# One queue for the feed-forward traffic, and the last column block's gradients moved into attention

## The chip, the cores and the metric

The kernel runs on one core of a Trainium2 chip. A core has five engines that run side by side, each through its own list of instructions in order: TensorE (PE in the profile; its weight loads are PEld), VectorE (DVE), ScalarE (ACT), GpSimd (POOL) and SyncE (SP, which only issues DMAs here). An engine waits for others through semaphores. DMAs are issued by SP, ACT or POOL and carried out by 16 DMA engines. Matrix products go to PSUM, which the DMAs do not touch here: DVE or ACT copies a result out of it ("evicts" it), and until then the bank cannot take the next product.

The metric is the device time of one execution, in microseconds. Before the change it was 905.26 us, the median of three runs (904.66 to 910.99).

## The reference

The forward pass mixes two branches of one input `x` (2048 rows, 512 columns, bfloat16) by a learned gate, and the kernel returns its output and all gradients for a given `grad_out`:

```python
g = sigmoid((x * gate_w).sum(-1, keepdims=True))
a = attention(x, wqkv) @ wo      # 32 heads of 16, causal, window of 256
b = (where(gate > 0, gate, 0) * up) @ W_down   # gate = x @ W_gate, up = x @ W_up
out = g * a + (1 - g) * b
```

Outputs are `out` (out_0), the gradient of x (out_1), of wqkv (out_2), wo (out_3), W_gate (out_4), W_up (out_5), W_down (out_6) and gate_w (out_7). The feed-forward width is F = 1376, which is ten blocks of 128 columns and 96 more.

Of the feed-forward branch the backward pass needs, for each block of columns, `h` (the product of the rectified gate and up), `dg` and `du` (the gradients at gate and up), then the weight gradients x^T dg, x^T du and h^T db, where db is `grad_out` times (1 - g), and later the sums over all blocks that make `b` and the gradient of x.

## The kernel before

The kernel has three stages, all written out in Python loops; in the first two the order of instructions on each engine is the order in which the code issues them.

**Feed-forward stage** (loop at L416). A step `k` is one block of 128 columns (`fc`, 11 of them) for one quarter of the rows (`tg`, 512 rows): 44 steps. The last block starts at F - 128 = 1248, so its first 32 columns repeat those of block 9. The parts of a step are issued with lags, so that iteration n does `gate` and `up` of step n, `dh` of step n-2, `turn_h` of n-1 (L362), `keep` of `hT` of n-3 and `turn_dgu` and `keep` of `dgT`, `duT` of n-4 (L366, L371), and `weights` of n-6 (L375).

- `gate`, `up` and `dh` are four matmuls of 512 columns each (L336). ACT rectifies (`rg`, L342) and copies `dh` (L356), DVE makes `upm` (L348) and `dg` (L359), POOL makes `h` (L350) and `du` (L360). In this form columns lie on partitions and rows along the free axis.
- `turn_h` and `turn_dgu` are DMA transposes on SP that bring rows onto the partitions for the weight gradients (`h_r` of 4 blocks of 128x128, `dgu_r` of 8).
- `keep` stores `h`, `dg` and `du` to three DRAM tensors `hT_d`, `dgT_d`, `duT_d`, by three DMAs on ACT's queue (L373), for the last stage.
- `weights` is 16 matmuls of 256 columns (L383, `wps`: both x^T dg and x^T du) and 4 of 512 (L385, `dps`), accumulated over the four quarters. After the fourth, ACT evicts one half of `wps` and all of `dps`, DVE the other half (L398 to L400, through the helper at L72 and L74), and three stores go out one iteration later. There is one `wps` buffer, so the next block's gradients wait for the eviction. For the last block, results go through a tile `wst_end` that attention's pool lends.
- Between these, from iteration 9 on, `make_da` and `turn_da` scale `grad_out` by g, store it as `da_d` and turn it, one row tile an iteration for sixteen iterations, on DVE and SP; and the attention projections of the first group are issued in the last iterations (L456 to L459).

In the built program each DMA on the queues of SP and ACT also waits for an earlier DMA: eight semaphores are given out in turn to the DMAs of both queues, in the order of issue in the code.

**Attention** (loop at L924). It goes through four column groups `c` of eight heads and, in each, through 46 turns. A turn makes scores S and their gradients' products D on PE (L666), exp on ACT (L699), masks on POOL (L709), the product with D on DVE (L716), row sums BA on PE (L733, L735), turns the probabilities either on PE (L770) with a copy by DVE or ACT or by a DMA transpose on SP (L762), and makes the CD products (L492, L495). PE's other work is spread over the turns as background jobs with a price in microseconds (`bg`, `jobs`, L995 to L1017): the projections of the next quarter of rows (L146), and from group 1 on the weight gradients of the group before (`grad_parts`, L564; matmuls at L599 and L602). At the start of each quarter of a group, `jobs` adds 0, 1, 2 or 2 jobs (L944). The gradients read rows of `da_d`, in pieces of two row tiles (`load_da`, L568): the first four are loaded by SP, the next four by ACT's queue (L604).

**Last stage** (loop at L1057): for each row tile the products that give `out` and the gradient of x, from what the first two stages have left in DRAM.

The lines that carry the change:

```python
            if at(1):
                turn_h(at(1))
            if at(3):
                keep(at(3), (hT_d, at(3).hT[:]))
            if at(4):
                turn_dgu(at(4))
                keep(at(4), (dgT_d, at(4).dgT), (duT_d, at(4).duT))
            if at(6):
                f = weights(at(6))
```

Of the kernel before, what the change touches and what calls it, by code (L numbers as in the profile page):

```python
# [22 lines left out]
def kernel(  # L23
# [100 lines left out]
    pjA = ctx.enter_context(tc.tile_pool(name="pjA", bufs=1))  # L124
    pjs = {}
    pools = {}

# [71 lines left out]

    with ExitStack() as p1, tc.manual_schedule():  # L200
# [7 lines left out]
        fp = p1.enter_context(tc.tile_pool(name="ffn", bufs=4))  # L208

# [98 lines left out]
        def make_da(t):  # L308
            da_t = fp.tile([P, D], BF, tag="da_t", bufs=2, name="da_t")
            nc.vector.tensor_scalar(da_t[:], go_in[t // TPG][:, t % TPG, :], g_all[:, t:t + 1], None, op0=ALU.mult)  # L310
            nc.sync.dma_start(da_d[t * P:(t + 1) * P, :], da_t[:])
# [32 lines left out]
        def up(k):  # L344
            ups = ps1.tile([P, TGW], F32, tag="mm", bufs=3, name="ups")
            product(ups, lambda c: Wu_sb[:, c, k.fsl], lambda c: x_T[k.tg][:, c, :])
            k.upm, k.hT = tile1("upm"), tile1("hT")
            nc.vector.scalar_tensor_tensor(out=k.upm[:], in0=k.rg[:], scalar=0.0, in1=ups[:],  # L348
                                           op0=ALU.is_gt, op1=ALU.mult)
            nc.gpsimd.tensor_tensor(out=k.hT[:], in0=k.rg[:], in1=k.upm[:], op=ALU.mult)  # L350

        def dh(k):
# [4 lines left out]
            k.dgu = fp.tile([P, 2, TGW], BF, tag="dgu", name="dgu")  # L357
            k.dgT, k.duT = k.dgu[:, 0, :], k.dgu[:, 1, :]
            nc.vector.tensor_tensor(out=k.dgT, in0=dh_sb[:], in1=k.upm[:], op=ALU.mult)  # L359
            nc.gpsimd.tensor_tensor(out=k.duT, in0=dh_sb[:], in1=k.rg[:], op=ALU.mult)  # L360

        def turn_h(k):  # L362
            k.h_r = fp.tile([P, TPG, P], BF, tag="h_r", bufs=6, name="h_r")
            nc.sync.dma_start_transpose(out=k.h_r[:], in_=k.hT[:])

        def turn_dgu(k):  # L366
            k.dgu_r = fp.tile([P, 2, TPG, P], BF, tag="dgu_r", name="dgu_r")
            nc.sync.dma_start_transpose(out=k.dgu_r[:].rearrange("p a t f -> p (a t) f"),
                                        in_=k.dgu[:].rearrange("p a s -> p (a s)"))

        def keep(k, *pairs):  # L371
            for dst, src in pairs:
                nc.scalar.dma_start(dst[k.fsl, k.ts], src)  # L373

        def weights(k):  # L375
# [14 lines left out]
            if k.fc < FC - 1:  # L390
                wst = fp.tile([P, DC, 2, P], BF, tag="wst", bufs=2, name="wst")
                dst = fp.tile([P, D], BF, tag="dst", bufs=2, name="dst")
                parts = [(0, wst[:, 0:h2, :, :]), (h2, wst[:, h2:DC, :, :])]
            else:
                end = wide("wst_end")[:].rearrange("p u a h q -> p (u a h q)")
                parts = [(c0, end[:, c0 * 2 * P:(c0 + h2) * 2 * P].rearrange("p (c a f) -> p c a f", c=h2, a=2)) for c0 in (0, h2)]
                dst = end[:, 2 * D:3 * D]
            for (c0, t), eng in zip(parts, ("act", "dve")):  # L398
                evac(t, v[:, c0:c0 + h2, :, :], eng)
            evac(dst[:], acc["d"][:], "act")  # L400

            def store():
                whole = parts if k.fc == FC - 1 else [(0, wst[:])]
                for a, to in ((0, out_4), (1, out_5)):
                    for c0, t in whole:
                        nc.sync.dma_start(to[:, k.fsl].rearrange("(c p) f -> p c f", p=P)[:, c0:c0 + t.shape[1], :], t[:, :, a, :])
# [755 lines left out]
```

## Time and profile before

| | |
|---|---|
| median of three runs | 905.26 us (904.66 to 910.99) |
| the profiled execution's own time, and its span | 910.07 us, 908.3 us |
| mean granted clock of TensorE in it | 0.987 |
| feed-forward stage on PE | from the start to 257.2 us |
| attention, start of its first and last exp | 258.9 and 707.2 us |

A profile is one execution. "Span" is the time from its first instruction to its last. Rows of the timeline give start and duration in us, the engine, the line, the operation, the tiles (written <- read), the count, and in brackets the idle time of the engine ahead of the row and what ended it. Rows of groups give busy time and mean duration in ns, then idle time. A "q" behind an engine's name marks its queue issuing a DMA. Busy times of PE overlap, since matmuls are pipelined: the distance from one start to the next is what a matmul costs.

### The profile page before, as it was taken

What the parts mean: (1) busy time and instruction counts of PE and PEld (TensorE: products, weight loads), DVE (VectorE), ACT (ScalarE), POOL (GpSimd) and SP (SyncE); (2) the same over time, 40 slices, a digit from 0 to 9 for tenths busy, and PEclk for the clock granted to TensorE, in tenths of its full rate; (3) what the DMA queues carried; (4) which work ended last, traced back from release to release, by engine and by line L of the source; (5) the groups of instructions that cost most, each with busy time, mean ns of one, the idle gap of its engine ahead of it and who ended that gap; (6) DMA issues with size and microseconds to landing.
All of it is one profiled execution on the core that took longest, in us unless ns stands there. A gap on an engine that the chain in (4) does not pass through costs nothing. (4 is left out here: it accounts for less than half of the span.)

```text
span 908.3 us, 29628 instructions
## 1 busy us (share of the span) xinstructions
PE 868.0 (96%) x12569; PEld 565.9 (62%) x12569; DVE 492.5 (54%) x754; ACT 390.0 (43%) x565; POOL 474.0 (52%) x883
## 2 busy tenths in 40 slices
PE   7999999999989999999999999999899999999998
PEld 4566555565657777776777767777577744444443
DVE  4543222233237888878778777788677323232322
ACT  5522222223246767675556655667465311111111
POOL 2544444454326877876668766687566512222221
PEclk9999999999988999999999999999899999999999
DMA  9989989989725999999987999999999999778750
GB/s 279 211 184 218 218 211 198 226 202 199 194 51 78 151 136 183 138 152 236 170 116 134 138 239 160 135 164 168 197 180 203 245 253 216 180 195 195 195 125 29
DMA packets 444334, 161.25 MB, mean 178 GB/s; under 512 B 362696, under 2 KB 441896, under 8 KB 444200
## 3 DMA queue, kind: packets, MB, share of 16 engines
q1 hardware_dynamic: 418520, 133.13, 81.5%
q10 hardware_dynamic: 23856, 20.98, 8.1%
q0 software_dynamic: 1824, 5.25, 1.6%
q8 instruction: 98, 1.61, 0.7%
q14 instruction: 36, 0.29, 0.1%
HBM read 38.44 MB, written 38.41 MB: 85 GB/s over the span
## 5 line engine op out<-in xcount | busy, mean ns | idle before, releaser
L716 DVE TENSOR_TENSOR PP<-PP,D 128x1024 bf16<-128x1024 bf16 (+1 forms) x184 | 219.6, 1193 | 69.6 <-POOL PP L709 24.9
L699 ACT ACTIVATE PP<-S 128x1024 bf16<-128x1024 f32 (+1 forms) x184 | 185.2, 1006 | 96.1 <-PE D L666 47.4
L709 POOL TENSOR_SCALAR_AFFINE_SELECT PP<-PP 128x512 bf16<-128x512 bf16 (+1 forms) x188 | 143.3, 763 | 109.9 <-ACT PP L699 94.6
L74 DVE COPY p<-pt 128x1024 bf16<-128x1024 bf16 x167 | 114.4, 685 | 17.4 <-PE pt L770 17.2
L770 PE MATMUL pt<-ident,PP 128*128 128x128 bf16 x1536 | 120.0, 224 | 1.6 <-DVE p L74 0.9
L350 POOL TENSOR_TENSOR hT<-rg,upm 128x512 bf16<-128x512 bf16 x44 | 52.5, 1193 | 127.1 <-DVE upm L348 103.0
L733 PE MATMUL BA<-KV,PP 128*128 128x33 bf16 x1440 | 106.9, 180 | 6.7 <-ACT BAs L72 6.7
L383 PE MATMUL wps<-dgu_r,x_r 128*128 128x256 bf16 x704 | 105.6, 273 | 4.3 <-DVE wst L74 3.9
L733 PEld LDWEIGHTS <-PP 128*128 128x128 bf16 x1440 | 85.9, 96 | 31.8 <-issue 12.2
L735 PE MATMUL BA<-KV,PP 128*128 128x17 bf16 x1440 | 102.4, 171 | 0.5 <-issue 0.5
L492 PE MATMUL CD<-rq,p 128*128 128x32 bf16 x1440 | 95.0, 176 | 0.0
L495 PE MATMUL CD<-rq,p 128*128 128x16 bf16 x1440 | 93.7, 169 | 1.2 <-issue 1.2
L735 PEld LDWEIGHTS <-PP 128*128 128x128 bf16 x1440 | 85.0, 97 | 14.7 <-issue 10.1
L770 PEld LDWEIGHTS <-PP 128*128 128x128 bf16 x1536 | 91.2, 100 | 1.8 <-issue 1.8
L383 PEld LDWEIGHTS <-x_r 128*128 128x128 bf16 x704 | 68.8, 98 | 36.2 <-issue 5.9
L666 PE MATMUL S<-zT,K 32*128 32x128 bf16 (+3 forms) x1056 | 78.3, 241 | 5.3 <-ACT PP L699 3.3
L495 PEld LDWEIGHTS <-p 128*128 128x128 bf16 x1440 | 80.6, 96 | 1.6 <-issue 1.3
L492 PEld LDWEIGHTS <-p 128*128 128x128 bf16 x1440 | 80.8, 96 | 0.3
L666 PE MATMUL D<-zT,V 32*128 32x128 bf16 (+3 forms) x1056 | 73.4, 240 | 4.3 <-DVE PP L716 3.8
L1074 ACT COPY a_sb<-aps 128x512 f32<-128x512 f32 x16 | 9.4, 586 | 145.9 <-issue 133.1
L348 DVE SCALAR_TENSOR_TENSOR upm<-rg,ups 128x512 bf16<-128x512 bf16 x44 | 30.2, 686 | 67.6 <-PE ups L336 43.0
L385 PE MATMUL dps<-db_r,h_r 128*128 128x512 bf16 x176 | 66.7, 379 | 0.0
(144 smaller groups left out, 1471.3 us busy)
## 6 DMA issues: line engine op xcount, KB each, us to landing
dqkvo_d<-rows_st SPq DMA_DIRECT2D x14, 512.0 KB, 4.7
hT_d<-hT ACTq DMA_DIRECT2D x44, 128.0 KB, 2.2
dgT_d<-dgu ACTq DMA_DIRECT2D x44, 128.0 KB, 2.8
duT_d<-dgu ACTq DMA_DIRECT2D x44, 128.0 KB, 2.8
duT_g<-duT_d SPq DMA_DIRECT2D x8, 640.0 KB, 5.9
dgT_g<-dgT_d SPq DMA_DIRECT2D x7, 640.0 KB, 5.6
gt<-hT_d SPq DMA_DIRECT2D x7, 640.0 KB, 6.0
dar<-da_d SPq DMA_DIRECT2D x16, 256.0 KB, 5.2
```

The lines of the kernel that those rows point to most:

```text
L74: nc.vector.tensor_copy(out, in_)
L383: nc.tensor.matmul(acc["w"][:, c, :], lhsT=x_r[:, t, c * P:(c + 1) * P], rhs=k.dgu_r[:, :, i, :], start=(go_ and c % 2 == 0), stop=no_, sk ...
L385: nc.tensor.matmul(acc["d"][:], lhsT=k.h_r[:, i, :], rhs=db_r[:, t, :], start=go_, stop=no_)
L492: nc.tensor.matmul(cd[0][:, h, :], lhsT=p2[:, 0, pr, :], rhs=rq[:, h, 0:2 * Dh], start=cd[1], stop=True, skip_group_check=True)
L495: nc.tensor.matmul(cd[0][:, h, 0:Dh], lhsT=p2[:, 1, pr, :], rhs=rq[:, h, 2 * Dh:3 * Dh], start=False, stop=True, skip_group_check=True)
L666: nc.tensor.matmul(dst, lhsT=proj[(u.c, kb // TPG)][nm + ("", "1")[par]][rows[par], (kb % TPG) * P:(kb % TPG + 1) * P], rhs=proj[(u.c, qb ...
L699: nc.scalar.activation(two[:].rearrange("p x a b q -> p x a (b q)")[:, :, 0, 0:n], flat(us[0].S[:], n), ACT.Exp)
L709: nc.gpsimd.affine_select(out=out, in_=out, compare_op=ALU.is_ge, fill=0.0, base=0 if up else -1, pattern=[[0, 2], [0, b1 - b0], [1 if up ...
L716: nc.vector.tensor_tensor(out=v(1), in0=v(0), in1=flat(vs[0].D[:], n), op=ALU.mult)
L733: nc.tensor.matmul(BA[:, h, 0:33], lhsT=u.PP[:, 0, 2 * i + pr, :], rhs=kv[:, kb % TPG, h, 1:34], start=(first and pr == 0), stop=True, ski ...
L735: nc.tensor.matmul(BA[:, h, 33:50], lhsT=u.PP[:, 1, 2 * i + pr, :], rhs=kv[:, kb % TPG, h, 0:17], start=False, stop=True, skip_group_check ...
L770: nc.tensor.transpose(pt[:, a, b if u.nb == 2 else 2 * u.x + b, :], u.PP[:, a, b, :], ident[:])
```

## The change

- `h`, `dg` and `du` of a step lie in one tile `hgu` (five buffers, in a pool of its own on the right side of the memory), are turned by one DMA transpose of 12 blocks and stored by one DMA into one DRAM tensor `hgu_d`, both on SP, three iterations after the step's `gate` (`weights` stays at six).
- ACT's queue issues only the first loads: the stores above and `load_da` are on SP. The store of `da_t` is issued just ahead of its transpose, one iteration later than before.
- The last block (fc = 10) is not given to `weights`. Its `h` is turned into a tile `h_end` of attention's pool, its `dg` and `du` into four tiles `dgu_end` that share buffers with the `da` rows, and `tail_parts` makes its gradients as three background jobs in attention's group 0: `down` (16 matmuls of 512 columns) and two times `up_gate` (32 matmuls of 192 columns, for the 96 new columns of two matrices). Group 0 takes 2 jobs in its first quarter and 1 in its second.
- `db_r` and `db_T`, which the first stage makes, lie in the two buffers that attention uses for `rows_st`.
- The pool of turned blocks `P2` is opened after turn 2 of attention, in the place of the `hgu` pool, which is closed there. In the first two row tiles of group 0, the pairs from the fourth on (k >= 3) are turned by DMA instead of PE.

```diff
-    hT_d = dram.tile([F, S], BF, name="hT_d")
-    dgT_d = dram.tile([F, S], BF, name="dgT_d")
-    duT_d = dram.tile([F, S], BF, name="duT_d")
+    hgu_d = dram.tile([3, F, S], BF, name="hgu_d")
+    hT_d, dgT_d, duT_d = (hgu_d[a] for a in range(3))
...
+    def rows_tile(name):
+        return st.tile([P, NT, 4, P], BF, tag="rows_st", name=name)
...
-        db_r = ap1.tile([P, NT, D], BF, name="db_r")
-        db_T = ap1.tile([P, DC, S], BF, name="db_T")
+        db_T = rows_tile("db_T")[:].rearrange("p t a n -> p (t a n)").rearrange("p (c s) -> p c s", c=DC)
+        db_r = rows_tile("db_r")[:].rearrange("p t a n -> p t (a n)")
...
+        fl = fend.enter_context(tc.tile_pool(name="ffnl", bufs=4, side="right"))
...
         def turn_da(t):
+            nc.sync.dma_start(da_d[t * P:(t + 1) * P, :], da_in[t][:])
             nc.sync.dma_start_transpose(out=da_T[t // TPG][:, :, (t % TPG) * P:(t % TPG + 1) * P], in_=da_in[t][:])
...
+        def turn(k, a0, a1, out):
+            nc.sync.dma_start_transpose(out=out, in_=k.hgu[:, a0:a1, :].rearrange("p a s -> p (a s)"))
+
         def turn_h(k):
-            k.h_r = fp.tile([P, TPG, P], BF, tag="h_r", bufs=6, name="h_r")
-            nc.sync.dma_start_transpose(out=k.h_r[:], in_=k.hT[:])
+            if k.tg == 0:
+                acc["h"] = wide("h_end")[:].rearrange("p u a h q -> p (u a) h q")
+            k.h_r = acc["h"][:, k.tg, :, :]
+            turn(k, 0, 1, k.h_r)
 
         def turn_dgu(k):
-            k.dgu_r = fp.tile([P, 2, TPG, P], BF, tag="dgu_r", name="dgu_r")
-            nc.sync.dma_start_transpose(out=k.dgu_r[:].rearrange("p a t f -> p (a t) f"),
-                                        in_=k.dgu[:].rearrange("p a s -> p (a s)"))
-
-        def keep(k, *pairs):
-            for dst, src in pairs:
-                nc.scalar.dma_start(dst[k.fsl, k.ts], src)
+            if k.fc < FC - 1:
+                r = fp.tile([P, 3, TPG, P], BF, tag="hgu_r", name="hgu_r")
+                k.h_r, k.dgu_r = r[:, 0, :, :], r[:, 1:3, :, :]
+                turn(k, 0, 3, r[:].rearrange("p a t f -> p (a t) f"))
+            else:
+                r = gwp.tile([P, 2, D], BF, tag="dar", bufs=4, name="dgu_end")
+                k.dgu_r = r[:].rearrange("p a (t f) -> p a t f", f=P)
+                turn(k, 1, 3, r[:].rearrange("p a (t f) -> p (a t) f", f=P))
+
+        def keep(k):
+            nc.sync.dma_start(hgu_d[:, k.fsl, k.ts].rearrange("a f s -> f a s"), k.hgu[:])
...
-            if at(1):
+            if at(1) and at(1).fc == FC - 1:
                 turn_h(at(1))
-            if at(3):
-                keep(at(3), (hT_d, at(3).hT[:]))
-            if at(4):
-                turn_dgu(at(4))
-                keep(at(4), (dgT_d, at(4).dgT), (duT_d, at(4).duT))
-            if at(6):
+            for lag, end in ((3, False), (3, True)):
+                if at(lag) and (at(lag).fc == FC - 1) == end:
+                    turn_dgu(at(lag))
+                    keep(at(lag))
+            if at(6) and at(6).fc < FC - 1:
...
-                    ev.setdefault(turn + 1, []).append(("load", lambda: load_da(t0 // 2 + 4, nc.scalar)))
+                    ev.setdefault(turn + 1, []).append(("load", lambda: load_da(t0 // 2 + 4)))
...
+        def tail_parts():
+            ends = steps[-NTG:]
+            lo = FC * P - F
+            new = FC * P - lo - (FC - 1) * P
...
+                for t in range(t0, t0 + step):
+                    nc.tensor.matmul(hold["d"][:], lhsT=ends[t // TPG].h_r[:, t % TPG, :], rhs=db_r[:, t, :], start=(t == 0), stop=(t == NT - 1))
...
+                    for c in range(2):
+                        nc.tensor.matmul(hold[h][:, c, :, :], lhsT=x_r[:, t, (2 * h + c) * P:(2 * h + c + 1) * P],
+                                         rhs=ends[t // TPG].dgu_r[:, :, t % TPG, lo:P], start=(t == 0 and c == 0), stop=(t == NT - 1),
+                                         skip_group_check=True)
...
-                        u.dma = x == 0 and len(blocks) == 2 and (c > 0 or q > 0) and (c < DC - 1 or q < NT - 2)
+                        u.dma = x == 0 and len(blocks) == 2 and (c > 0 or q > 0 or k >= 3) and (c < DC - 1 or q < NT - 2)
...
-            jobs = []
+            jobs = tail_parts()
...
-                        for _ in range((0, 1, 2, 2)[j // TPG]):
+                        for _ in range(((2, 1, 0, 0) if c == 0 else (0, 1, 2, 2))[j // TPG]):
...
+                if turn == 2:
+                    fend.close()
+                    pools["p2"] = p3b.enter_context(tc.tile_pool(name="attp2", bufs=2, side="right"))
```

More of the change, by code (lines that the diff above doesn't have):

```diff
@@ L198, in project_parts @@
             return out
+    fend = ExitStack()
     with ExitStack() as p1, tc.manual_schedule():
@@ L389, in weights @@
             v = acc["w"][:].rearrange("p c (a f) -> p c a f", a=2)
[L390 to L399, printed above, removed]
+            wst = fl.tile([P, DC, 2, P], BF, tag="wst", bufs=2, name="wst")
+            dst = fl.tile([P, D], BF, tag="dst", bufs=2, name="dst")
+            for c0, eng in ((0, "act"), (h2, "dve")):
+                evac(wst[:, c0:c0 + h2, :, :], v[:, c0:c0 + h2, :, :], eng)
             evac(dst[:], acc["d"][:], "act")
             def store():
-                whole = parts if k.fc == FC - 1 else [(0, wst[:])]
                 for a, to in ((0, out_4), (1, out_5)):
-                    for c0, t in whole:
-                        nc.sync.dma_start(to[:, k.fsl].rearrange("(c p) f -> p c f", p=P)[:, c0:c0 + t.shape[1], :], t[:, :, a, :])
+                    nc.sync.dma_start(to[:, k.fsl].rearrange("(c p) f -> p c f", p=P), wst[:, :, a, :])
                 nc.sync.dma_start(out_6[k.fsl, :], dst[:])
@@ L937 @@
                     if j == 0:
-                        sts[c] = st.tile([P, NT, 4, P], BF, tag="rows_st", name="rows_st")
+                        sts[c] = rows_tile("rows_st")
                     if j % TPG == 0:
```

53 lines of the change are left out of this document (39 added, 14 removed).

## The prediction

> **What bounds the kernel now.** I read the page first: busy shares and the granted clock.
>
> ```profile
> PE 868.0 (96%) x12569; PEld 565.9 (62%) x12569; DVE 492.5 (54%) x754; ACT 390.0 (43%) x565; POOL 474.0 (52%) x883
> PEclk9999999999988999999999999999899999999999
> ```
>
> TensorE is busy nearly throughout, ACT less than half the time, and the clock dips near slices 13 and 29, which is where attention begins and late in it. A busy PE need not be at its peak, so next the timeline of PE in the feed-forward stage.
>
> ```profile
> 150.81 1.03 PE L336 MATMUL gps<-x,Wg_sb 128*128 128x512 bf16 x4
> 151.67 1.03 PE L336 MATMUL ups<-x,Wu_sb 128*128 128x512 bf16 x4
> ...
> 156.02 1.02 PE L336 MATMUL gps<-x,Wg_sb 128*128 128x512 bf16 x4
> ```
>
> Four 512-column matmuls start 0.86 us after the four before (151.67 - 150.81), 0.215 us each, and a whole step takes 156.02 - 150.81 = 5.21 us. A step is 16 matmuls of 512 columns and 16 of 256, or 24 x 0.215 = 5.16 us. So a step runs at PE's own pace, and only work taken from PE, or a stall taken from it, shortens this stage. The waits of PE from 45 to 257 us list all its stalls:
>
> ```profile
> PE wps L383 <- DVE wst L74: 3.9, 4, 1.2
> PE wps L383 <- DMA dgu_r<-dgu: 0.3, 1, 0.3
> ```
>
> Of attention, windows over the same 34 turns of column group 0 (which has no weight gradients in the background) and group 1 (which has them), then that group's rows:
>
> ```profile
> 289.60:364.00 74.40, 72.56 (x1833) 57.57 (x1832) 65.68 (x95) 51.71 (x67) 59.21 (x133) 1.00 1.07 156
> 389.70:478.40 88.70, 85.39 (x1914) 63.38 (x1915) 67.69 (x95) 52.94 (x73) 60.81 (x135) 1.00 1.04 167
> L599 PE MATMUL wps<-rows_st,x_r 128*128 128x384 bf16 x64 | 12.0, 326 | 0.6 <-ACT ws L72 0.6
> ```
>
> Columns after the window are its length, then PE, PEld, DVE, ACT, POOL, clock, DMA share and GB/s. Group 1 is 14.3 us longer. What it has more is 64 matmuls of 384 columns and 16 of 512: 32,768 columns. That is 0.436 ns a column, against 0.215 us / 512 = 0.42 at peak. So PE bounds attention too, and background work costs its full price there: nothing hides it, though DVE (88% in the first window) is not far behind.
>
> **The change part by part.**
>
> *The last block's gradients leave the first stage.* Before, they are the last thing on PE ahead of attention:
>
> ```profile
> 245.24 1.03 PE L146 MATMUL pp<-x,p 128*128 128x512 bf16 x4
> 246.36 0.60 PE L383 MATMUL wps<-dgu_r,x_r 128*128 128x256 bf16 x4
> ...
> 258.38 0.39 PE L666 MATMUL S<-zT,K 16*128 16x256 bf16 x4 [1.19 <-DVE wst_end L74]
> 246.31 0.59 ACT L72 CAST V<-pp 128x512 bf16<-128x512 f32 x1 [0.23 <-PE pp L146]
> 249.40 0.42 DVE L74 COPY KV<-ptp 128x512 bf16<-128x512 bf16 x1 [2.12 <-PE ptp L184]
> ```
>
> Up to V's projection (PE, 245.24) the order on PE stays. Then before runs 16 groups of gradients until 257.2, with V's transposes among them. After, nothing covers V's eviction: it ends at 246.90, four transposes take some 0.4 us (until 247.4), and the first S waits for the copy of their result, 0.42 us, as the built program has it. S comes at about 247.9 instead of 258.38: **-10.5 us**. The bounds of this term are -10.5 - 1.2, if V comes as promptly as it did with cover, and -10.5 + 2, if the evictions of block 9 (1.2 us on ACT) go first. I take -10.5.
>
> *They come back in attention.* 16 matmuls of 512 columns, and 64 of 192 (only the 96 new columns of each matrix) instead of 64 of 256: 20,480 columns x 0.436 = **+8.9 us**. In the first turns three units of eight blocks are turned by DMA instead of PE:
>
> ```profile
> 270.76 1.05 PE L770 MATMUL pt<-ident,PP 128*128 128x128 bf16 x16
> 257.20:261.50 4.30, 1.93 (x18) 0.69 (x19) 1.50 (x2) 3.04 (x5) 0.69 (x2) 1.00 0.35 92
> 261.50:268.30 6.80, 6.53 (x78) 4.71 (x77) 3.75 (x6) 4.31 (x6) 2.80 (x6) 0.50 0.00 0
> 268.30:275.20 6.90, 5.50 (x110) 3.79 (x108) 5.10 (x6) 5.05 (x6) 3.86 (x8) 0.99 0.01 2
> 275.20:282.00 6.80, 6.43 (x92) 4.94 (x92) 3.71 (x7) 3.76 (x5) 2.91 (x10) 0.50 0.19 36
> 282.00:289.60 7.60, 7.10 (x168) 5.40 (x165) 6.58 (x9) 6.50 (x9) 5.73 (x12) 1.00 0.68 95
> ```
>
> 24 transposes at (1.05 - 0.2) / 15 = 0.057 us: **-1.4 us**. The windows cover the first twelve turns. PE idles 4.9 us there (32.4 less 27.5 busy), waiting for exp and for copies; the gradients and the now faster projection of the next group (four matmuls a turn, not two) stand in these holes. I take half: **-2.5 us** (bounds 0 and -4.9). Two stretches run at a granted clock of 0.50. I leave them as they are; bounds below. The evictions move with the work (three on DVE or ACT before, three after) and DVE loses three copies, so they cost nothing extra.
>
> A new wait: the pool of turned blocks now takes the place of the step buffers, and its first copy on DVE waits for the last store of block 9. Queued behind it on DVE are the products that feed the row sums, and PE behind these. In the old trace that copy, POOL's last product and the median landing of a block's last store are
>
> ```profile
> 263.82 0.68 DVE L74 COPY p<-pt 128x1024 bf16<-128x1024 bf16 x1
> 243.32 1.39 POOL L360 TENSOR_TENSOR dgu<-dh_sb,rg 128x512 bf16<-128x512 bf16 x1 [2.95 <-ACT dh_sb L356]
> out_dram<-dst SPq DMA_DIRECT2D x10, 128.0 KB, 2.7
> ```
>
> The copy comes 5.4 us after the first S (263.82 - 258.38). From POOL's end at 244.7 SP issues a transpose and four stores (3.4 us by its rows below), and the last lands 2.7 us later, at 250.8: 3 us after S. So I count nothing; without that slack the price is up to 3 us.
>
> *ACT issues no DMAs after the loads.* This is how a stall arises, in order on ACT, DVE and PE:
>
> ```profile
> 96.19 0.33 ACTq L373 DMA_DIRECT2D hT_d<-hT  x1
> ...
> 97.59 0.59 ACT L72 CAST wst<-wps 128x512 bf16<-128x512 f32 x1 [4.10 <-PE ups L336]
> 98.21 0.69 DVE L74 CAST wst<-wps 128x512 bf16<-128x512 f32 x1 [3.79 <-ACT wst L72]
> 98.95 0.49 PE L383 MATMUL wps<-dgu_r,x_r 128*128 128x256 bf16 x3 [0.89 <-DVE wst L74]
> ```
>
> ACT had been idle for 4.10 us, yet the eviction stood behind a step's three stores (the first is shown), issued from 96.19 on, which waited for their data and for earlier DMAs. Without them it follows its matmuls at once: 0.59 on ACT and 0.69 on DVE, against 2.6 us of products (three times 0.86) before PE needs the bank. The stalls of L383, 3.9 + 0.3, go: **-4.2 us**. What is late next is DVE behind `da_t`, which waits for a DMA from SP; SP's load falls, as shown below.
>
> The same in attention, in group 3, where ACT issued the loads of `da` rows; the same six turns of group 2 stand ahead as a measure:
>
> ```profile
> 643.23 0.43 ACTq L572 DMA_DIRECT2D dar<-da_d  x1
> 643.76 1.02 ACT L699 ACTIVATE PP<-S 128x1024 bf16<-128x1024 f32 x1 [4.09 <-DMA rows<-zT]
> 645.22 0.19 PE L733 MATMUL BA<-KV,PP 128*128 128x33 bf16 x1 [3.40 <-ACT BAs L72]
> 519.00:533.40 14.40, 13.48 (x337) 10.12 (x336) 11.82 (x16) 6.91 (x9) 10.15 (x23) 1.00 1.17 227
> 633.30:651.80 18.50, 15.10 (x342) 11.13 (x339) 12.09 (x16) 6.91 (x9) 10.85 (x24) 0.82 1.21 212
> ```
>
> The load held up exp by 4.09 us, PE idled 3.40 us, and the clock fell to 0.82 of full over these turns: 18.5 against 14.4 us, **-4.1 us** when the load is SP's.
>
> The Trainium skill's "DMA: Bandwidth & Descriptors", section "Issuing engines are not separate DMA queues", says that issuing from several engines only saves the sequencer's issue time. Read strictly it speaks against both terms: the moved DMAs would give ACT back issue time it has to spare, and the sum would lose 4.2 and 4.1 us. The rows above show that ACT also stands still while a DMA waits to be issued, so I keep both; the strict reading is rival 2.
>
> *One transpose and one store a step, on SP.*
>
> ```profile
> 145.04 1.22 SPq L364 DMA_TRANSPOSE h_r<-hT  x1
> 146.30 1.31 SPq L368 DMA_TRANSPOSE dgu_r<-dgu  x1
> 148.93 0.51 SPq L407 DMA_DIRECT2D out_dram<-dst  x1
> 200.00:225.00 25.00, 25.00 (x157) 15.21 (x156) 7.72 (x11) 6.99 (x12) 12.13 (x10) 1.00 0.94 201
> ```
>
> A transpose of 4 blocks takes 1.22 us to issue, of 8 blocks 1.31. One of 12 is not in the trace: at most three times 1.22 = 3.7, at least 1.31; I take 1.4, by the step from 4 to 8. With a store (0.5) and, in the sixteen steps that turn `da`, a store and a transpose (0.5 + 1.2), SP issues for 3.6 us of a 5.21 us step, where before it was 4.2 without ACT's three stores. The transpose is issued three steps after its matmuls and read three steps later, 15 us, so its landing stays hidden.
>
> **The sum.** -10.5 + 8.9 - 1.4 - 2.5 - 4.2 - 4.1 = -13.8 us. Against the profiled execution's own 910.07 us (span 908.3) that is 896.3. The runs were 904.66, 905.26 and 910.99, so the profiled one is 4.8 above the median, about the size of the group 3 event. If the faster runs lacked that event, the sum for them is -9.7, from 905.26: 895.6. Both ways about **896**.
>
> **The rivals.**
>
> 1. *The clock stays up at the start of attention.* PE is denser there after the change. Each stretch of 6.8 us at 0.50 does 3.4 us of work; without both, 6.8 us less: 889. For it: the share of PE busy in the window before the first drop was 1.93 of 4.30, and more matmuls now stand there. Against it: the chain S, exp, S is the same, and PE newly waits for V. By the skill's "TensorE: Matmul & The Clock Gate", section "Why this matters for your kernels", the clock falls after idle gaps of over about 3 us; the trace agrees at the 3.40 us gap, but the first drop had no gap above 1.19 us, so here the measurement decides.
> 2. *The moves only give back issue time* (the change doesn't do what it says). The stalls stay, as the chain ACT, DVE, PE still stands at each block's end, and half of the 8.9 us falls into the halved stretches, +4.5: 896 + 4.2 + 4.5 = 905. Against it is the idle ACT in the rows above.
> 3. *SP holds up attention.* A `da` load that waits now blocks the transposes behind it, and their blocks are late for CD on PE. At the 4.1 us of the group 3 event in each of three groups: 896 + 12.3 = 908. Against it: no wait of PE for those transposes stood out.
> 4. *Slower: the transfers of the first stage.* The DMA share there is 0.94, and the same bytes pass. If joined transposes and stores took the DMA engines more time, steps would last as long as DMA does: from 6% on the engines are full, and at 20% more a step is 5.21 x 0.94 x 1.2 = 5.88, +0.67 for 44 steps = 29 us, less the 10 us that the three steps' lead absorbs after landing: 915. Against it: `dgu_r`, twice the blocks, issues like `h_r` and nothing shows it hold the queue longer.
>
> **How the numbers follow.** My forecast of 896 gets 0.46, with 891 to 901 as its own range; rival 1 gets 0.18, rival 2 0.16, rival 3 0.09, rival 4 0.11. The range, 887 to 911, leaves out rival 4 and the far side of rival 1, about 2 in 10. One per cent, about what a measurement here can tell from no change, is 9.05 us: below 896.2 is faster. Half of the forecast (0.24) and rival 1 with some of its neighbours (0.2) make 0.44; rival 4 and a little of rival 3 make 0.13 slower; the rest, 0.43, is within.
>
> **What the changed profile would show.** Steps of 5.21 us without a wait of `wps` for `wst`; the first S some 15 us earlier, near 243.7; the `h_end` and `dgu_end` matmuls within the first two dozen turns; group 0 about 5 us longer from its first S to group 1; no wait of ACT for a DMA in group 3, and the same length for its turns as in group 2. I am wrong if steps exceed 5.21 us, if PE waits for `hgu_r`, if DVE waits long at its first copy of a turned block, or if the halved stretches grow to three.

## The result and the profile after

| | before | after |
|---|---|---|
| median of the runs | 906.80 us (904.66 to 910.99, 6 runs) | 897.02 us (892.31 to 901.73, 6 runs) |
| the profiled execution, its span | 910.07 us, 908.3 us | 901.73 us, 900.0 us |
| first S | 258.4 us | 242.2 us |
| from there to exp of turn 12 | 31.2 us | 29.8 us |
| from there to group 1's first exp | 74.5 us | 77.5 us |
| group 1, group 2, group 3 (to its last exp) | 114.4, 114.7, 114.1 us | 115.8, 116.3, 113.2 us |
| from there to the last stage's first product, and to the end | 26.6, 174.5 us | 25.9, 179.3 us |

The ratio is 0.989, with a 95% interval of 0.985 to 0.993. So the kernel became about 1.1% faster, against a forecast of 896. The sum came out nearly right while two of its reasons were not; that is what the experiments are about. Line numbers move by 4 to 46: `wps` is L383 before and L397 after, `pt` L770 and L816.

Two rows of the page after, busy times and the granted clock by slices:

```profile
PE 851.1 (95%) x12420; PEld 559.8 (62%) x12545; DVE 500.4 (56%) x755; ACT 387.2 (43%) x561; POOL 475.4 (53%) x883
PEclk9999999999999999999999989999999999999999
```

The dip at attention's start is gone. This trace lacks 125 matmul records (12420 of PE against 12545 weight loads), so PE's busy time in it is a little low. The feed-forward stage by the timeline of PE: first `gate` of two steps, then the end of the stage; rows of ACT and DVE from their timelines stand last.

```profile
151.81 1.03 PE L342 MATMUL gps<-x,Wg_sb 128*128 128x512 bf16 x3
157.01 1.03 PE L342 MATMUL gps<-x,Wg_sb 128*128 128x512 bf16 x4
...
239.56 1.03 PE L150 MATMUL pp<-x,p 128*128 128x512 bf16 x4
241.27 0.40 PE L188 MATMUL ptp<-ident,V 128*128 128x128 bf16 x4 [0.68 <-ACT V L72]
242.18 0.40 PE L712 MATMUL S<-zT,K 16*128 16x256 bf16 x4 [0.52 <-DVE KV L74]
...
240.63 0.59 ACT L72 CAST V<-pp 128x512 bf16<-128x512 f32 x1 [0.23 <-PE pp L150]
...
241.71 0.42 DVE L74 COPY KV<-ptp 128x512 bf16<-128x512 bf16 x1
```

A step is 5.20 us, and PE's waits between 45 and 255 us no longer have a row of `wps` for `wst`. V's projection comes at 239.56 where it came at 245.24, 5.7 us sooner, and from it to the first S it is now 2.62 us, before 13.14: 10.5 us less.

Attention by windows: the first twelve turns; the other 34 turns of group 0; the same 34 of group 1; and two windows in group 3.

```profile
241.20:272.00 30.80, 26.64 (x477) 18.84 (x481) 20.67 (x29) 18.74 (x26) 16.28 (x35) 1.00 0.67 113
272.00:349.50 77.50, 73.75 (x1850) 59.74 (x1864) 66.59 (x96) 51.64 (x67) 59.41 (x133) 1.00 1.03 146
374.50:465.40 90.90, 84.58 (x1903) 63.55 (x1917) 68.22 (x96) 52.95 (x73) 60.73 (x136) 1.00 0.99 163
...
631.40:634.80 3.40, 1.98 (x64) 1.66 (x65) 1.54 (x4) 0.73 (x1) 1.37 (x5) 1.00 1.11 254
634.80:638.20 3.40, 3.04 (x61) 2.37 (x59) 1.83 (x3) 0.99 (x2) 1.37 (x3) 0.50 1.09 175
```

PE's two largest waits for another engine from 255 to 700 us (total, times, longest):

```profile
PE wps L604 <- DMA dar<-da_d: 5.3, 4, 2.2
PE D L712 <- DVE PP L762: 4.0, 12, 0.6
```

And the longest of the first kind on PE's timeline:

```profile
632.76 0.38 PE L604 MATMUL wps<-dar,rows_st 128*128 128x512 bf16 x1 [2.20 <-DMA dar<-da_d]
```

Group 0 got only 1.6 us longer (29.8 + 77.5 against 31.2 + 74.5). The new row is PE's wait for `dar`, the loads that went from ACT's queue to SP's; half clock follows the longest of them. The last stage is 4.8 us longer in this one profile, with a wait of 2.60 us for a transpose. In the profiles of all twelve kernels below it takes 174.5 to 175.6 us, and ten of the twelve have after's last stage, so I count it as chance.

### The profile page after: what moved, and what is told of

Read it like the earlier page. It is cut to its first block, busy times and chain, and to the rows that moved or that the text cites. A ratio compares the mean times of both kernels' runs of the same rounds, so it can differ in the third digit from the quotient of the medians.

```text
span 900.0 us, 29247 instructions
## 1 busy us (share of the span) xinstructions
PE 851.1 (95%) x12420; PEld 559.8 (62%) x12545; DVE 500.4 (56%) x755; ACT 387.2 (43%) x561; POOL 475.4 (53%) x883
## 5 line engine op out<-in xcount | busy, mean ns | idle before, releaser
L74 DVE COPY p<-pt 128x1024 bf16<-128x1024 bf16 x167 | 114.4, 685 | 17.3 <-PE pt L816 17.1
L816 PE MATMUL pt<-ident,PP 128*128 128x128 bf16 x1512 | 115.1, 219 | 2.0 <-issue 2.0
L357 POOL TENSOR_TENSOR hgu<-rg,upm 128x512 bf16<-128x512 bf16 x44 | 51.2, 1165 | 120.2 <-DVE upm L355 99.9
L779 PEld LDWEIGHTS <-PP 128*128 128x128 bf16 x1440 | 85.6, 96 | 30.8 <-issue 11.5
L397 PE MATMUL wps<-hgu_r,x_r 128*128 128x256 bf16 x640 | 96.0, 273 | 0.7
L781 PEld LDWEIGHTS <-PP 128*128 128x128 bf16 x1440 | 84.8, 96 | 9.6 <-issue 5.0
L816 PEld LDWEIGHTS <-PP 128*128 128x128 bf16 x1512 | 86.8, 97 | 2.2 <-issue 2.2
L397 PEld LDWEIGHTS <-x_r 128*128 128x128 bf16 x640 | 62.6, 98 | 28.6
L365 POOL TENSOR_TENSOR hgu<-dh_sb,rg 128x512 bf16<-128x512 bf16 x44 | 58.3, 1325 | 9.0 <-ACT dh_sb L363 9.0
```

Of the source, the lines that this page charges most:

```text
L74: nc.vector.tensor_copy(out, in_)
L397: nc.tensor.matmul(acc["w"][:, c, :], lhsT=x_r[:, t, c * P:(c + 1) * P], rhs=k.dgu_r[:, :, i, :], start=(go_ and c % 2 == 0), stop=no_, sk ...
L779: nc.tensor.matmul(BA[:, h, 0:33], lhsT=u.PP[:, 0, 2 * i + pr, :], rhs=kv[:, kb % TPG, h, 1:34], start=(first and pr == 0), stop=True, ski ...
L781: nc.tensor.matmul(BA[:, h, 33:50], lhsT=u.PP[:, 1, 2 * i + pr, :], rhs=kv[:, kb % TPG, h, 0:17], start=False, stop=True, skip_group_check ...
L816: nc.tensor.transpose(pt[:, a, b if u.nb == 2 else 2 * u.x + b, :], u.PP[:, a, b, :], ident[:])
```

## The experiments

Each is timed beside the kernel before, whose median was 905.8 to 908.0 us there; ratios are to it. "After" stands for the changed kernel.

### The moved block

**block10_first** is after with the last block's gradients back in the first stage.

```diff
-            if k.fc < FC - 1:
+            if True:
                 r = fp.tile(...)
-            if at(1) and at(1).fc == FC - 1:
-                turn_h(at(1))
-            if at(6) and at(6).fc < FC - 1:
+            if at(6):
-            jobs = tail_parts()
+            jobs = []
-    for _ in range(((2, 1, 0, 0) if c == 0 else (0, 1, 2, 2))[j // TPG]):
+    for _ in range((0, 1, 2, 2)[j // TPG]):
```

> The changed kernel with one part undone: the last block's gradients are made in the first stage again, like those of the other blocks (no background jobs for them in attention; the joined transpose and store stay). My theory: the first S comes 10.5 us later, at about 252.7; attention's first group is shorter by the 8.9 us of background work less the 2.5 us of idle time that it filled, and the clock is halved again in the first turns because PE is thin there, up to 6.8 us. So 901 without the halving, up to 908 with it. Rival: background work has its full price and the clock is chance, so the move was worth nothing but the repeated columns (4096 columns, 1.8 us): 897 to 899.

It took 900.88 us (897.22 to 901.65), ratio 0.9935 [0.991, 0.996]. The first S comes at 252.0, 9.8 us later than after; the next twelve turns take 25.65 us instead of 29.81 (with 6.83 us at half clock in them, of which after has none), the rest of group 0 takes 74.50 instead of 77.53. So the move takes 9.8 us out of one stage and puts 7.2 into the other: 2.6 us by the profiles, 3.9 by the medians.

**flips_on_pe** is after with the three early units turned on PE again.

```diff
-  u.dma = x == 0 and len(blocks) == 2 and (c > 0 or q > 0 or k >= 3) and (...)
+  u.dma = x == 0 and len(blocks) == 2 and (c > 0 or q > 0) and (...)
```

> The changed kernel with the three early units of blocks turned on PE and copied again, as before the change, in place of DMA transposes. By the prediction's term PE gets 24 transposes of 0.057 us back: +1.4 us, 898.4, seen in the length of the first twelve turns (29.8 to about 31). Rival: these turns wait for exp, not for PE, so that the transposes fall into idle PE and the length stays within 0.5 us; a stretch at half clock then is no likelier, or even less likely, since PE is denser.

899.18 us (895.94 to 902.70), ratio 0.9922 [0.9896, 0.9948]. Its first twelve turns in a window:

```profile
241.20:275.20 34.00, 28.14 (x501) 1.00 0.42 78
```

Against 30.80 us and 26.64 busy in after, 3.2 us come back, of which 1.5 are PE's work (the forecast's 1.4) and 1.7 are idle time. Among it are waits of PE for copies of turned blocks that after does not have: 1.0 us of `pt` for DVE, 0.9 of `ptp` for ACT. By the profiles the term was half of its worth; by the medians (2.2 us) it was two thirds.

### Who issues the stores

**store_on_act** is after with the joined store back on ACT's queue.

```diff
-  nc.sync.dma_start(hgu_d[:, k.fsl, k.ts].rearrange("a f s -> f a s"), k.hgu[:])
+  nc.scalar.dma_start(hgu_d[:, k.fsl, k.ts].rearrange("a f s -> f a s"), k.hgu[:])
```

> The changed kernel with the joined store of h, dg and du on ACT's queue instead of SP's; nothing else differs. My theory (the issue on ACT's queue is what held up the eviction): waits of PE's weight gradients for the eviction come back, 4 us in four places, and the time rises to about 901. Rival: it was not the queue as such but three stores a step in a shared row of eight semaphores, with loads that came late; a single store three iterations after its step finds its data ready and holds up nothing: no such wait, 897.

897.50 us (896.29 to 899.00), ratio 0.9913 [0.9893, 0.9934]; no stall of `wps`. So a store of each step on ACT's queue does no harm, and my reason for the 4.2 us fell. Three differences from before were left: three stores instead of one, two transposes instead of one, and the lag.

**three_stores_on_act** has three stores a step on ACT, as before.

```diff
-  nc.sync.dma_start(hgu_d[:, k.fsl, k.ts].rearrange("a f s -> f a s"), k.hgu[:])
+  for a in range(3):
+      nc.scalar.dma_start(hgu_d[a, k.fsl, k.ts], k.hgu[:, a, :])
```

> The changed kernel, but a step's h, dg and du are stored by three DMAs on ACT's queue (same lag of three steps, same joined transpose on SP), the same work in all. Theory A, the number of DMAs: with three stores a step more of the eight shared semaphores are in use at once, a store waits for an earlier DMA and holds ACT's evictions, and the stalls of wps for wst come back: about 4 us, 901. Theory B, the wait was for the data of the later products (the old order stored dg and du a step later than h and beside the four separate transposes): with three stores behind one joined transpose no stall returns, 897 (895 to 899), as with the joined store on ACT's queue (897.5).

894.72 us (894.41 to 899.09), ratio 0.9874 [0.9824, 0.9924]; no stall of `wps` either. The number of stores isn't it.

**split_all_on_act** is that kernel with the joined transpose split in two as well: as many DMAs a step as before.

```diff
-  turn(k, 0, 3, r[:].rearrange("p a t f -> p (a t) f"))
+  turn(k, 0, 1, k.h_r)
+  turn(k, 1, 3, k.dgu_r.rearrange("p a t f -> p (a t) f"))
```

> The changed kernel with the joining undone alone: a step's h and its dg, du turned by two DMA transposes on SP, stored by three DMAs on ACT's queue, as many DMAs a step as before (lag three steps for all). In the trace of before each late store on ACT is issued within 0.02 us of the landing of a transpose or of a load that SP had issued (118.34 after 118.32, 141.26 after 141.24). Theory A (SP's late queue, felt by ACT through the shared semaphores): the extra transpose, 1.2 us of SP's issue a step, makes SP late in the steps that turn da, and the four stalls of wps for wst come back: about 4 us, 899 to 901. Theory B (it was the lag or the order of the stores): no stall, 895 to 897.

908.05 us (905.28 to 910.40), ratio 1.0014 [0.9993, 1.0034]: of the change's gain nothing is left. The waits of PE from 45 to 255 us:

```profile
PE wps L399 <- DVE wst L74: 7.1, 5, 2.5
```

One of these waits on the timelines of SP, ACT and PE:

```profile
96.44 2.59 SPq L368 DMA_TRANSPOSE hgu_r<-hgu  x2
99.12 0.88 SPq L320 DMA_DIRECT2D da_d<-da_t  x1
100.06 1.23 SPq L321 DMA_TRANSPOSE d<-da_t  x1
...
98.41 1.63 ACTq L389 DMA_DIRECT2D hgu_d<-hgu  x3
100.16 0.58 ACT L72 CAST wst<-wps 128x512 bf16<-128x512 f32 x1 [3.93 <-PE dhps L342]
...
101.53 0.60 PE L399 MATMUL wps<-hgu_r,x_r 128*128 128x256 bf16 x4 [2.37 <-DVE wst L74]
```

ACT stands idle for 3.93 us ahead of the eviction, with three stores issued just before it, as in the trace of before. The first S comes at 252.9, 9.8 us later than in three_stores_on_act (243.1). The lag is three steps in both, so what removes the stalls is one transpose in place of two on SP. The trace of before shows how SP's transposes get at ACT. A transpose on SP's timeline and the stores on ACT's:

```profile
115.53 1.31 SPq L368 DMA_TRANSPOSE dgu_r<-dgu  x1
...
118.34 0.33 ACTq L373 DMA_DIRECT2D hT_d<-hT  x1
118.71 0.47 ACTq L373 DMA_DIRECT2D dgT_d<-dgu  x1
119.22 0.46 ACTq L373 DMA_DIRECT2D duT_d<-dgu  x1
119.78 0.59 ACT L72 CAST wst<-wps 128x512 bf16<-128x512 f32 x1 [4.44 <-PE ups L336]
```

The DMA view of a window around that transpose, with the time from issue to landing in us:

```profile
dgu_r<-dgu SPq DMA_TRANSPOSE x1, 2.8
```

The transpose lands at 118.3, and ACT issues its store in that moment, as it does at 96.19, 122.90 and 141.26 (landings at 96.17, 122.88 and 141.24): the store follows a DMA of SP's queue. The trace names the link: each of these four stores carries one wait, and it is for the semaphore on which just that DMA of SP lands (numbers 110 at 96.19 and 118.34, 109 at 122.90, 104 at 141.26). It is one of the eight that the two queues share, and the store signals the same one when it lands. In split_all_on_act the store at 98.41 follows a landing at 98.39 in the same way (number 102). The eviction waits behind. So ACT was late because SP was. No run took the sharing away.

**before_stores_on_sp** is the kernel before with its three stores a step on SP, the opposite half of the change.

```diff
-                nc.scalar.dma_start(dst[k.fsl, k.ts], src)
+                nc.sync.dma_start(dst[k.fsl, k.ts], src)
```

> The old kernel with its three stores a step issued on SP instead of ACT, nothing else changed. Theory A (ACT's queue is what held the evictions): the four stalls of wps for wst (4.8 us in the profile with the loads moved) go, about 902 against 906.5. Theory B (the three stores and two transposes fill SP's issue: 2.5 us for the transposes, 1.5 us for the stores, and in sixteen steps 1.7 us and more for da, together 5.7 us of a 5.21 us step): PE waits for dgu_r or h_r in these steps instead, and the first S comes later than 258; 907 or more.

948.08 us (944.60 to 949.38), ratio 1.0442 [1.0400, 1.0484]. Waits of PE from 45 to 255 us:

```profile
PE wps L383 <- DMA dgu_r<-dgu: 19.9, 20, 5.1
PE ups L336 <- DVE upm L348: 8.8, 4, 3.0
```

SP's timeline, from one step's `h_r` to the next one's:

```profile
112.71 1.20 SPq L364 DMA_TRANSPOSE h_r<-hT  x1
113.95 0.58 SPq L373 DMA_DIRECT2D hT_d<-hT  x1
114.58 1.23 SPq L368 DMA_TRANSPOSE dgu_r<-dgu  x1
...
121.81 1.21 SPq L364 DMA_TRANSPOSE h_r<-hT  x1
```

The window from 60 to 195 us, in the columns of the windows above:

```profile
60.00:195.00 135.00, 110.64 (x620) 63.12 (x631) 28.92 (x59) 28.41 (x49) 45.34 (x40) 0.95 0.64 167
```

SP has a DMA in issue nearly without a break and needs 9.1 us for this step (121.81 - 112.71), which ends a block and turns `da`; 1.83 us of it are a store of `da` that takes 0.40 in the next step, so a wait may be in it. The DMA engines are busy for 0.64 of this window, in before for 0.97, while PE waits for transposes. SP's issue is a resource of its own, and the first S comes 41 us late (299.4). Up to 8.5 us of the 41 (an estimate) are the clock, which is at 0.50 for 17.1 us ahead of it. The Trainium skill's "DMA: Bandwidth & Descriptors", section "Issuing engines are not separate DMA queues", says that another issuing engine saves only the time to initiate a DMA, usually small beside the DMA. The first half agrees with the runs above, where the issuing queue of the stores made no measurable difference. The second is true here of one store (0.43 to 0.59 us to issue, some 2 us until it lands), but not of their sum on one queue, which cost the 41 us.

### Who issues the loads of `da`

**before_da_on_sp** is the kernel before with only the second four loads on SP.

```diff
-  ev.setdefault(turn + 1, []).append(("load", lambda: load_da(t0 // 2 + 4, nc.scalar)))
+  ev.setdefault(turn + 1, []).append(("load", lambda: load_da(t0 // 2 + 4, nc.sync)))
```

> The kernel before with only the second four loads of da rows moved from ACT's queue to SP's. By the prediction's term this alone gains the group 3 event, 4.1 us: 902 to 903 against 906.8. By the profile of the changed kernel it trades that event for waits of PE for the loads of 1 to 2 us a group, and the clock falls after these too: 906 to 908.

909.77 us (904.80 to 913.82, 10 runs), ratio 1.0038 [1.0013, 1.0062]: a little slower, not 4 us faster. **da_on_act** is the reverse, after with these loads on ACT; **da_on_pool** has them on POOL, and **da_now** on SP, but issued in the turn that frees the buffer.

```diff
-  ev.setdefault(turn + 1, []).append(("load", lambda: load_da(t0 // 2 + 4)))
+  ev.setdefault(turn + 1, []).append(("load", lambda: load_da(t0 // 2 + 4, nc.scalar)))  # da_on_act
+  ev.setdefault(turn + 1, []).append(("load", lambda: load_da(t0 // 2 + 4, nc.gpsimd)))  # da_on_pool
+  load_da(t0 // 2 + 4)                                                                   # da_now
```

> The changed kernel with the second four loads of da rows in groups 1 to 3 on ACT's queue, as before the change. By the prediction the exp behind such a load is held up again and PE idles 3.4 us in group 3: 901. By the profile of the changed kernel the loads on SP stand behind transposes and come late (PE waits 2.1, 1.0 and 2.2 us for them in groups 1, 2 and 3, and the clock halves twice right after): without these waits 5 us less, and up to 5 us more where the clock stays up: 887 to 892. If both hold, they cancel: 897.

> The changed kernel with the second four loads of da rows issued on POOL's queue, so that neither SP's transposes nor ACT's exp stand beside them in order. Theory A: the waits of PE for dar (5.3 us) go and nothing takes their place, also fewer stretches at half clock follow: 890 to 892. Theory B: the load waits on POOL for its buffer as it did on ACT, and holds up POOL's masks behind it, so that PE waits for D or BA instead: 896 to 899, as on ACT's queue (894.6).

> The changed kernel with the second four loads of da rows issued in the turn in which the piece before has freed the buffer, not one turn later; on SP as in the changed kernel. Theory A: the loads come one turn (2.4 us) earlier, the waits of PE for dar (5.3 us, longest 2.2) fall to about 1, and the half clock after the longest of them with them: 891 to 894. Theory B: on SP the load then waits for its piece ahead of the transposes of the same turn, so blocks come late for CD, or the load waits for a semaphore anyway: no gain, 896 to 898.

They took 894.63 (894.58 to 900.44), 898.63 (895.51 to 907.11) and 896.69 us (896.59 to 899.42); ratios 0.9897 [0.9863, 0.9931], 0.9912 [0.9881, 0.9943] and 0.9891 [0.9866, 0.9917], all within each other's intervals and after's: in time the four placements cannot be told apart. PE's largest waits in attention, first of before_da_on_sp, then of da_on_act, da_on_pool and da_now in turn:

```profile
PE wps L602 <- DMA dar<-da_d: 4.8, 4, 2.5
```

```profile
PE BA L779 <- ACT BAs L72: 8.9, 14, 3.0
```

```profile
PE S L712 <- ACT PP L745: 5.7, 10, 2.9
PE wps L604 <- DMA dar<-da_d: 2.2, 4, 0.9
```

```profile
PE wps L604 <- DMA dar<-da_d: 6.7, 4, 2.2
```

In these single profiles the wait changes its name: on SP, PE waits for the load; on ACT, evictions are held (2.6 us of that row in after, 8.9 here); on POOL the wait for the load shrinks and one for exp grows (2.8 us in after, 5.7 here; its cause was not traced). Where the load is late shows in the issue of group 3's first two loads, of after, da_on_act and da_now in turn (the loads that open the group stand at 594.9, 595.3 and 595.0, so the three are in step):

```profile
629.66 1.04 SPq L574 DMA_DIRECT2D dar<-da_d  x2
```

```profile
624.49 0.96 ACTq L574 DMA_DIRECT2D dar<-da_d  x2
```

```profile
630.05 1.04 SPq L574 DMA_DIRECT2D dar<-da_d  x2
```

On SP, behind its transposes, the load is issued 5.2 us later than on ACT. The transfer itself is not slower there: 3.2 us from issue to landing on SP (the second of the two), 4.6 and 4.8 on ACT. And da_now did not bring the load forward: in the code it stands a turn earlier, in time it is issued at 630.05. So what an earlier load would gain was not tested.

On ACT, PE's waits for these loads are 0.8 us in all. What is held there is the fourth load of group 3: it waits, as the stores of the first stage did, for a semaphore of SP's queue (a transpose that SP issues at 625.23 and that lands at 632.22; the load follows at 632.32), and ACT's work stands behind it. That this must be so on ACT is not shown: queues_back below has its loads on ACT too, no wait of PE for `dar` at all, and

```profile
PE BA L780 <- ACT BAs L72: 3.7, 12, 1.1
```

Whether a fifth buffer of rows would end the wait wasn't tried.

### The parts by themselves

**queues_back** is after with ACT's queue as before: three stores a step and the loads of `da` on ACT (the edits of three_stores_on_act and da_on_act together). **join_alone** is that with the edits of block10_first and flips_on_pe besides: of the whole change, only the joined transpose with its tiles and lag is left, and with it the places in memory and the later store of `da_t`, which no run took back.

> The changed kernel with ACT's queue as before the change: three stores a step and the second four loads of da rows on ACT; the joined transpose, the moved block and the early DMA transposes stay. Theory A (which queue issues is worth nothing; the joined transpose and the moved block carry the gain): 893 to 897, the changed kernel's time or a little less, no wait of wps for wst. Theory B (ACT's free queue carries a part of the gain): 900 or more, with waits of ACT's evictions behind stores and of exp behind loads.

> As the run with ACT's queue as before, and besides the last block's gradients back in the first stage and the three early units of blocks back on PE: against the old kernel only the joined transpose of a step (with its tiles and its lag of three) is left. Theory A: the stalls of wps go and the first S comes some 6 us earlier (252), the rest as before: 899 to 902 against 906.5; the other 3 to 6 us of the change are then the moved block's. Theory B: without ACT's queue free the stalls stay, 905 to 907.

queues_back: 894.43 us (890.09 to 895.46), ratio 0.9837 [0.9804, 0.9870]. join_alone: 903.37 us (897.72 to 908.34, 12 runs), ratio 0.9952 [0.9925, 0.9979]. Neither has a stall of `wps` for `wst` in the blocks. So the joined transpose alone, with the little that stays beside it, is worth 2 to 7 us, the moved block with the early DMA transposes 9 us on top (903.37 - 894.43), and the part that the change began with, ACT's queue kept free, nothing or a small loss: queues_back has the lowest median of all, 0.2 us below da_on_act. It beats before; its lead of 2.6 us over after is within after's spread.

The sizes do not simply add up. The moved block is worth 3.9 us in one pair, 9 less some 2 for the early transposes in another, and without the joining nothing: split_all_on_act has it and takes as long as before. Joining, in turn, is worth 13.3 us where the block is moved (908.05 - 894.72). In part this is because two transposes with the lag of three stall PE longer than the old order did (7.1 us against 3.9); the rest was not traced. The granted clock is another reason. Windows about the first S, first of join_alone and then of queues_back:

```profile
252.60:256.00 3.40, 1.58 (x16) 0.54 (x16) 0.69 (x1) 2.12 (x4) 0.38 (x1) 1.00 0.35 70
256.10:262.90 6.80, 6.29 (x67) 4.37 (x66) 4.56 (x6) 4.37 (x7) 2.08 (x4) 0.50 0.06 20
```

```profile
245.80:249.20 3.40, 2.19 (x34) 1.54 (x34) 2.57 (x3) 2.33 (x4) 1.28 (x2) 0.99 0.28 54
249.20:252.60 3.40, 3.40 (x32) 1.87 (x31) 1.08 (x3) 1.91 (x4) 0.23 (x1) 0.51 0.02 5
```

With the block in the first stage, PE is busy for 1.58 us of 3.40 when attention starts, and half clock follows. All five profiles of that kind (before, block10_first, before_da_on_sp, before_stores_on_sp, join_alone) have half clock in the first twelve turns; of the nine with the block moved one has, queues_back, for 3.4 us. So the moved work does keep the clock up, as far as one profile of each kernel can show it.

## Why the prediction was right, and where it was not

- **V to the first S, -10.5:** right, -10.5 (13.14 to 2.62 us); block10_first gives 9.8 back.
- **The stalls of `wps`, -4.2:** the size was near, the cause wrong. V's projection comes 5.7 us earlier; 0.7 of it is there at 38 us already (a `gate` starts at 38.1 before and at 37.4 after), and 5.0 are the longer steps at the block ends (a row of waits counts idle time alone). But the step "without them it follows its matmuls at once" named the wrong culprit: with three stores a step on ACT no stall comes back, and with two transposes on SP they are back, and longer (7.1 us). The term belonged to the joined transpose, which I had booked as a cost on SP and no more. The transpose's size held: 1.27 to 1.44 us to issue, by these rows of after's SP timeline, against my 1.4. The joined store takes 0.89 us, where I had 0.5.

```profile
97.81 1.27 SPq L368 DMA_TRANSPOSE hgu_r<-hgu  x1
...
141.46 1.44 SPq L368 DMA_TRANSPOSE hgu_r<-hgu  x1
142.94 0.89 SPq L387 DMA_DIRECT2D hgu_d<-hgu  x1
```

- **Block 10 in attention, +8.9 - 1.4 - 2.5 = +5.0:** measured +1.6 for group 0. The early transposes were worth 3.2 us rather than 1.4 (flips_on_pe). The holes did not fill: PE's idle time over the first twelve turns went from 4.9 to 4.2 us (30.80 - 26.64), and with those transposes on PE it is 5.9, so the moved work itself filled none that can be seen. What closes the sum is the clock, which I had left as it was. In the two windows of before at 0.50 PE was busy for 6.53 and 6.43 us; at the full clock that is half the time, so 6.5 us are gone (an estimate). 8.9, less 1.5 of PE's work in the transposes, less 6.5, is 0.9 of the 1.6 measured; the other 0.7 was not traced. That is rival 1, at nearly its price of 6.8.
- **The event in group 3, -4.1:** wrong. ACT's wait of 4.1 us for a DMA is gone as I said, but "the same length for its turns as in group 2" is not so. The same six turns of after, in group 2 and in group 3, by windows:

```profile
505.50:518.90 13.40, 12.97 (x334) 10.14 (x334) 11.65 (x16) 6.91 (x8) 10.12 (x23) 1.00 1.07 219
622.50:639.40 16.90, 14.08 (x335) 10.87 (x338) 11.98 (x16) 6.89 (x8) 10.77 (x24) 0.90 1.21 182
```

They take 16.9 us, with the clock at 0.90, where group 2 takes 13.4. The step that failed is "when the load is SP's", which let the load's lateness vanish with its engine. On SP the load comes out behind transposes, 5.2 us later than on ACT, and PE waits for it: 5.3 us in all in after, 4.8 in before_da_on_sp, 6.7 in da_now. I had also put down to ACT what came from SP: the load at 643.23 in before had waited for the semaphore of a transpose of SP that landed at 643.13, the `rows<-zT` of the row I showed. Groups 1 to 3 together got 2.1 us longer.
- **Costs set at nothing:** DVE's first copy of a turned block starts at 247.4 without a wait, PE never waits for `hgu_r` after 45 us, and steps are 5.20 us.
- **The rivals:** rival 1 came for the most part. Its reading of the one long gap is not quite so: in before the clock fell at 643.81, when the gap of 3.40 us (641.82 to 645.22) was 2.0 us old. Rival 2 was half right, and the strict reading of the Trainium skill with it: the queue that issues is worth nothing (queues_back), yet the stalls went, by the joining. Its price was also short, since it kept the 4.1 us of group 3, which its own premise takes away. Rival 3 had the place (a `da` load on SP) but not the form: PE waits for the load itself, 5.3 us instead of 12.3. Rival 4 did not come; a joined transpose lands in 3.9 us and a joined store in 3.8, by the rows of the DMA view from 140 to 190 us of after, well inside the three steps of lead:

```profile
hgu_d<-hgu SPq DMA_DIRECT2D x10, 384.0 KB, 3.8
...
hgu_r<-hgu SPq DMA_TRANSPOSE x10, 3.9
```

By the profiles the sum is -16.2 at the first S, +1.6 in group 0, +2.1 in groups 1 to 3, -0.7 at attention's end and +4.8 in the last stage: with rounding -8.3, from 908.3 to 900.0. Without the last, chance term it is -13.1, against -13.8 forecast. That the total stood is luck: groups 1 to 3 missed by 6.2 us one way, and the first stage (1.5), group 0 (3.4) and attention's end (0.7) by about as much the other. The clock and the early transposes gave what the loads of `da` did not.

## What to carry to other kernels

When an engine stands still behind its own DMA issue, look at what lands in the moment it goes on: here it was a DMA of another queue, and the cure was fewer issues there, not moving the stores. Add up a queue's issue time per step like an engine's busy time, and join transfers whose issue costs nearly the same whatever their size (here the transposes). A load that is moved to another queue stands behind what that queue already issues and may come later there, so a wait that goes should be booked as a gain only when it is said what has become earlier.

## What the runs showed that I had not expected

- **A transpose's issue costs by the instruction, hardly by its size.** One of 4, 8 and 12 blocks takes 1.2, 1.3 and 1.3 to 1.4 us of SP. A store's costs more with its size, but less than in proportion: 0.3 to 0.6 us for 128 KB, 0.9 for 384 KB. Putting three stores of 0.4 to 0.6 us a step on SP cost 41 us, with the DMA engines at 0.64.
- **The clock follows how densely PE is fed, more than single gaps.** I cut all fourteen traces, from 45 us on and without their last 3 us, into windows of 3.41 us, laid on the start of the first stretch at half clock of each. Of 45 falls to half clock (without the one at each trace's end), 42 followed a window in which PE was busy for under 2.35 us, and 35 under 2.0; of 3386 windows that no fall followed, 47 and 9 were that thin. So under 2.0 us a fall follows four times in five, and between 2.0 and 2.35 it mostly doesn't. The largest gap inside the window was under 2 us in 34 of the 45. The Trainium skill's "TensorE: Matmul & The Clock Gate", section "Why this matters for your kernels", puts the fall at idle gaps of more than about 3 us; here several short gaps within 3.41 us were enough, as in join_alone, whose longest was 1.19 us at the first S.
